# Window attention with a mixture of experts: heads transposed ahead of rows, the first slot's rows split at once, expert weights loaded from step 5

## The chip, the cores and the metric

The kernel runs on one core of a Trainium2 chip. The metric is device time in microseconds. Time before: 641.11 us, the median of three runs (640.95 to 641.42).

## The reference

Attention with a causal window of 64 positions feeds a mixture of eight experts, of which each token uses one.

```python
B, H, S, D = (8, 8, 576, 64)
scores = np.matmul(q, k.transpose(0, 1, 3, 2)) / np.sqrt(D)
scores = np.where((rel >= 0) & (rel < 64), scores, -1e9)     # rel = i - j
attn = softmax(scores)
x = np.matmul(attn, v).transpose(0, 2, 1, 3).reshape(4608, 512)
logits = x @ w_gate + modality_bias[modality_id]             # 8 experts
e_idx, gate_w = argmax(logits), max(softmax(logits))
for e in range(8):
    mask = e_idx == e
    out[mask] = gate_w[mask, None] * (np.maximum(x[mask] @ w1[e], 0) @ w2[e])
```

w1 is 512 x 1024 and w2 is 1024 x 512 for each expert, all in float32.

## The kernel before

The 4608 positions are 72 blocks of 64. A step s (0 to 35, and four more that drain) does one pair of blocks for all eight heads; two pairs make a group G, whose q and k are transposed together. The work of a pair is spread over four steps. In step s TensorE (PE) does, in this order: the values of pair s-2 (`values`, L633), the logits of pair s-3 (`logits`, L658), the scores of pair s (`scores`, L581), two transpositions of the probabilities of pair s-1 (`probs_t`), the transposition of the attention rows of pair s-2 (`x_t`, from `xa` to `xaT`), and two transpositions of heads for the next group (`heads_t`: K in even steps, Q in odd ones). All transpositions carry the line of a helper, L439. In odd steps from 5 on the routing's matrix products follow (`route2`).

VectorE (DVE) does the copy of the upper half of v (L511), the sums' reciprocal, `xa` (L641), the bias of the logits (`lg`, L663), eight masked minima (L595), the copies of the heads out of PSUM (L546), the small routing operations, which a queue hands out a few at a time (`tick`), and `split_lo` (L116). ScalarE (ACT) does the copies of the transposed probabilities (`pT`, L616), eight exponentials (L607) in three portions of two, three and three, the copy `xaT` (L650) behind the first portion, the copy of the heads K1, and `split_hi` (L111). GpSimd scatters the finished rows to DRAM by expert. SP issues nearly all loads.

From step FIRST = 12 on, the experts run between the attention's parts. Work of one expert on up to 256 rows is a slot; `slot_pieces` is a generator that yields after each piece of a slot, and `gap(it, True)` in a step takes one piece. The first two pieces of a slot transpose its rows, which come from DRAM (`x_part`, L254); then come products in float32 taken apart into a high and a low part (`first`, L279; `second`, L301). What a piece leaves to be done on ScalarE and VectorE stands in a list, `later`, and runs where `run_later()` is called: for `x_part` the split into `xh` (L192) and `xl` (L193), for `first` the split into `hh` and `hl`.

The weights of the two experts that are used first come in 32 pieces of 256 KB. Which experts these are is worked out on VectorE (`choose`, L783) and read into registers of SP (`load_weights`, L799). Each call of `weights(s)` does at most three things: the low part of the piece whose high part the call before made, the high part of the older of two loaded pieces, and the load of the next, so that two are always on their way:

```python
if halves:
    split_lo(*halves.pop(0))
if len(raws) == 2 or raws and not pieces:
    split_hi(*raws[0])
```

PSUM has banks `tp` (two), `sp0`, `sp1`, `av`, `em`, `y0` and `y1`. `turn_bank(s)` hands out the transpositions' banks: before step 12 in turn `tp`, `tp`, `em`, `y0`, `y1`, then the two `tp` alone. In step 0 a second pair of transpositions is needed for group 0 (`first_pair(1, ...)`), whose copies the scores of step 1 wait for. The k and q of groups 1 to 7 wait in a stretch of SBUF that later holds weights, and so are named `Whi` in rows.

The order is written by hand in the loop over steps: each engine works through what the loop gives it, in that order.

Of the kernel before, what the change touches and what calls it, by code (L numbers as in the profile page):

```python
# [8 lines left out]
F32 = mybir.dt.float32  # L9
# [10 lines left out]
P = 128  # L20
# [6 lines left out]
def tile_window_attn_moe(  # L27
# [12 lines left out]
    nc = tc.nc  # L40
# [8 lines left out]
    NPR = NBLK // 2  # L49
# [14 lines left out]
    FIRST = 12  # L64
# [56 lines left out]
    queue = []  # L121
# [4 lines left out]
    def tick(n=1, table=False):  # L126
        for _ in range(n):
            if routing and not table:
                routing.pop(0)()
            elif queue:  # L130
                queue.pop(0)()
                issued[0] += 1
# [94 lines left out]
    def run_later():  # L227
        while later:
            later.pop(0)()

    def fetch():
        if fetched:
            return fetched.pop(0)
        row, late, buf, whichever, need = todo.pop(0)
        assert late is not None or not pads
        assert late is None or late in scattered
        tick(need - issued[0], table=True)
        nb = 1 if whichever == NANY else 2
        return dict(xt=load_slot(row, late, nb), buf=buf, any=whichever, nb=nb)
# [191 lines left out]
    def gap(it, wait=False):  # L431

        if next(it, "end") != "end" and not wait:
            run_later()
            tick()
# [10 lines left out]
    ps_m = actx.enter_context(tc.tile_pool(name="ps_m", bufs=1, space=PSUM))  # L446
# [36 lines left out]
    def turn_bank(s):  # L483

        i = n_tp[0]
        n_tp[0] += 1
        if s < FIRST and i % 5 > 1:
            return ps_m.tile([P, 512], F32, name=("em", "y0", "y1")[i % 5 - 2])
        return ps_t.tile([P, 512], F32, name="tp")
# [45 lines left out]
    def heads_t(G, nm, i, tp):  # L535


        src = qk[G, nm].rearrange("p t (h a) d -> p t h (a d)", a=2)
        for h in range(2):
            for t in range(2):  # L540
                n = 2 * h + t
                turn(tp[:, n * P:(n + 1) * P], src[:, t, 2 * i + h])

    def heads_out(tp, G, nm, i, copy):
        dst = by_group(qT if nm == "q" else kT)[:, G % 2, 2 * i:2 * i + 2]
        copy(out=dst.rearrange("p h j (i t) -> p h t (j i)", t=2),  # L546
             in_=tp.rearrange("p (h t i) -> p h t i", h=2, t=2))
# [54 lines left out]
    def exps(p, us):  # L602
        ss, mn, sm = st[p, "s"]
        for u in us:
            a, hp = divmod(u, HP)
            h = 2 * hp + a
            nc.scalar.activation(  # L607
                out=ss[a][:, hp, :], in_=ss[a][:, hp, :], func=AF.Exp,
                bias=mn[:, h:h + 1], scale=-1.0, accum_out=sm[:, h:h + 1])
# [35 lines left out]
    def x_t(p, xp):  # L645
        xa = st[p, "xa"]
        for c in range(NC1):
            turn(xp[:, c * P:(c + 1) * P], xa[:, c * P:(c + 1) * P])
        xaT = st[p, "xT"] = work.tile([P, DM], F32, name="xaT")
        nc.scalar.copy(out=xaT, in_=xp)  # L650

    def logits(p, lt):
        G, j = divmod(p, GB)
        xaT = st.pop((p, "xT"))
        for c in range(NC1):
            for i in range(2):
                cols = slice(c * P + i * W64, c * P + (i + 1) * W64)
                nc.tensor.matmul(  # L658
                    out=lt[i * W64:(i + 1) * W64, 0:E], lhsT=xaT[:, cols], rhs=wg[:, c, :],
                    start=(c == 0), stop=(c == NC1 - 1))  # L660
        if j == 0:
            st[G, "lg"] = small.tile(sh3, F32, name="lg")
        nc.vector.tensor_tensor(  # L663
            out=st[G, "lg"][:, j, :], in0=lt[:, 0:E], in1=bias_sel[:, p, :], op=ALU.add)
# [118 lines left out]
    def choose():  # L783

        lead = []
        for m in range(2):
            c = brow[0:1, m, :]
            u, _, mx = first_max(tab, f"selb{m}", c)
            rest = stt(tab, f"rest{m}", u, -1.0e6, c, ALU.mult, ALU.add)
            less = reduce(tab, f"less{m}", rest, ALU.max)  # L790
            lead.append(tt(tab, f"lead{m}", mx, less, ALU.subtract))
            if m:
                cnt0 = ts(tab, f"cnt0_{m}", u, lead[m], ALU.mult)
                cnt0 = stt(tab, "cnt0", last_u, lead[0], cnt0, ALU.mult, ALU.add)
            last_u = u
        pick("X", 0, cnt0)
        pick("Y", 1, stt(tab, "cnt1", sel2[:, 0, :], -1.0e6, cnt0, ALU.mult, ALU.add))

        def load_weights():  # L799
            for x in range(2):  # L800
                evs.append(nc.values_load(ix2[0:1, x:x + 1], engines=[ET.SP], min_val=0, max_val=E - 1))
            pieces.extend((x, c) for x in range(2) for c in PIECE_ORDER)
        queue.append(load_weights)


    at = {}
# [52 lines left out]
    for h in range(2):  # L859
        rows = slice(h * W64, (h + 1) * W64)  # L860
# [99 lines left out]
    def weights(s):  # L960
# [5 lines that stand above are left out]
            halves.append(raws.pop(0))  # L966
        while pieces and len(raws) < 2:
            x, c = pieces.pop(0)
            raw = epool.tile([P, WCH], F32, name="y", bufs=4)
            raws.append((load_piece(raw, evs[x], c), x, c))  # L970

    for s in range(NPR + 4):
        j = s % GB
        for f, args in at.pop(s, ()):
            f(*args)
        n_tick = 6 if s < FIRST else 5
        n_gap = 0 if s < FIRST else 4
        G = s // GB + 1
        heads = PARTS[j] if G < NG else ()
        R = (s - 5) // GB if s >= 5 and j == 1 else -1  # L980
        if 1 <= s < FIRST:
            swap_upper(s - 1)

        if 2 <= s < NPR + 2:
            values(s - 2)
            values_out(s - 2)
        if 3 <= s < NPR + 3:
            logits(s - 3, turn_bank(s))
            if (s - 3) % GB == GB - 1:
                route1((s - 3) // GB)  # L990
        if s < NPR:
            scores(s)
            if s == 0:
                keep_warm(WARM[1])
            minima(s)
        if 1 <= s <= NPR:
            if s >= FIRST:
                swap_upper(s - 1)
            swap_v(s - 1)
            for a in range(2):  # L1000
                probs_t(s - 1, a, turn_bank(s))
            sums(s - 1)
        if s < NPR:
            exps(s, (0, 1))
        if n_gap > 0:
            gap(it, True)
        if 2 <= s < NPR + 2:
            x_t(s - 2, turn_bank(s))
        run_later()
        tick(2)  # L1010
        if s == FIRST - 1:
            fetched.append(fetch())
        if s < NPR:
            exps(s, (2, 3, 4))
        if s == 0:
            first_pair(1, (both[:1], both[1:]))
        if n_gap > 0:
            if s < FIRST + 4 or s % 2:
                weights(s)
            gap(it, True)  # L1020
        if heads:
            tp = turn_bank(s)
            heads_t(G, *heads[0], tp)
            heads_out(tp, G, *heads[0], nc.vector.tensor_copy)
        run_later()
        tick(n_tick)
        cnt = None
        if R >= 0:
            tp = turn_bank(s)
            rk = route2(R, tp)  # L1030
            if R == NG - 1 or any(R == T for T, _ in EARLY):
                cnt = counts_out(tab if R == NG - 1 else pl, counts(R, tp))
            route3(R, rk)
        if s < NPR:
            exps(s, (5, 6, 7))
        if n_gap > 2:
            if FIRST < s < FIRST + 3:
                weights(s)
            gap(it, True)
        if heads:  # L1040
            tp = turn_bank(s)
            heads_t(G, *heads[1], tp)
            heads_out(tp, G, *heads[1], nc.scalar.copy if heads[1] == K1 else nc.vector.tensor_copy)
        run_later()
        tick(n_tick)
        if s >= 3:
            weights(s)
        if n_gap > 3:
            gap(it, True)
        run_later()  # L1050
        if s == 0:
            choose()
        if s == 1:
            select_bias()
        if s == 4:
            nc.sync.dma_start(out=xs_blk[DUMMY:DUMMY + 2].rearrange("b p c -> p b c"), in_=padrow)
        for T, xs_ in EARLY:
            if T == R:
                plan(T, xs_, cnt)
# [120 lines left out]
    while next(it, "end") != "end":  # L1180
# [6 lines left out]
        for n in range(RAWS):  # L1187
            if n < len(swaps) and n == len(ahead) and swaps[n][0] <= t + RAWS:
                _, buf, x, c = swaps[n]
# [18 lines left out]
    with tc.If(trip > 0):  # L1208
        NS = N // P + E
        with ExitStack() as gctx:  # L1210
# [38 lines left out]
            with tc.For_i(0, trip, 1) as it:  # L1249
# [22 lines left out]
                for n in range(F // 512):  # L1272
                    tp = gps.tile([P, 512], F32, name="gxp")
# [53 lines left out]
```

## Time and profile before

| | |
|---|---|
| median of the runs | 641.11 us |
| the profiled execution | 641.34 us, its span 639.6 us |
| busy, share of the span | PE 616.7 us (96%), DVE 367.5 (57%), ACT 299.9 (47%), POOL 136.0 (21%) |
| granted clock of TensorE | 0.998 of full speed |
| DMA | 88.07 MB, mean 138 GB/s |
| scores begin | step 1: 14.48 us, step 12: 77.97, step 13: 90.62 |

The share of busy time is an average over two stages: the attention without slots, steps 0 to 11, and everything behind it. Rows of a timeline give an instruction's start, its duration, engine, line, operation and operands, and in brackets the time its engine had been idle and what ended that.

### The profile page before, as it was taken

How to read it: one execution, taken by the hardware profiler on the slowest of the kernel's cores; microseconds unless marked ns; L12 is line 12 of the kernel's file. 1: busy time of each engine (PE TensorE's matmuls, PEld its weight loads, DVE VectorE, ACT ScalarE, POOL GpSimd, SP SyncE). 2: the span in 40 equal slices, each digit the busy share in tenths (PEclk: the TensorE clock that was granted, in tenths of full speed). 3: DMA queues.
4: the chain of work that ended last, by engine and by line, in shares of the span. 5: the costliest groups of instructions: out<-in, count | busy, mean ns of one | idle time of the engine just before them, and what ended most of it. 6: DMA issues, size and time to landing. Idle time of an engine off the chain costs nothing.

```text
span 639.6 us, 17262 instructions
## 1 busy us (share of the span) xinstructions
PE 616.7 (96%) x6508; PEld 552.8 (86%) x6509; DVE 367.5 (57%) x1495; ACT 299.9 (47%) x933; POOL 136.0 (21%) x314
## 2 busy tenths in 40 slices
PE   6799889999999999999999999999999999999996
PEld 4687778989898899989888899998999889989885
DVE  2999968767677766666654364213224624667611
ACT  4799867665657555646462111111112513554411
POOL 5333232132212320321222121011001001101102
PEclk9999999999999999999999999999999999999999
DMA  9999975866677754563312026312232723678301
GB/s 162 207 233 231 187 196 132 198 171 159 149 171 176 156 134 85 133 149 85 101 50 101 34 100 244 113 41 67 61 136 78 241 79 111 204 245 242 104 1 36
DMA packets 138885, 88.07 MB, mean 138 GB/s; under 512 B 116746, under 2 KB 116784, under 8 KB 138672
## 3 DMA queue, kind: packets, MB, share of 16 engines
q1 hardware_dynamic: 130112, 67.44, 43.6%
q0 software_dynamic: 5856, 18.92, 8.0%
q10 hardware_dynamic: 2832, 0.59, 0.7%
q8 instruction: 52, 0.85, 0.6%
q14 instruction: 33, 0.27, 0.2%
HBM read 67.49 MB, written 23.91 MB: 143 GB/s over the span
## 4 chain that ended last, share of the span: by engine, by line
PE 50%; DVE 0%; ACT 0%; issue 0%; POOL 0%; POOLq 0%; ACTq 0%
PE y L301 23%; PE em L279 13%; PE sp L279 10%; PE tp L439 1%; PE y L352 1%; PE av L633 1%; PE em L254 1%; PE tp L254 1%; PE sp L327 0%; PE em L327 0%; PE tp L658 0%; PE sp L581 0%; DVE xa L641 0%; ACT ss L607 0%; POOL out_dram L365 0%
## 5 line engine op out<-in xcount | busy, mean ns | idle before, releaser
L301 PE MATMUL y<-Whi,hh 128*128 128x512 f32 x288 | 118.7, 412 | 0.0
L607 ACT ACTIVATE ss<-ss,mn 128x128 f32<-128x128 f32 x288 | 112.9, 400 | 4.5 <-DVE mn L595 4.5
L301 PE MATMUL y<-Wlo,hh 128*128 128x512 f32 x288 | 112.9, 392 | 0.0
L301 PE MATMUL y<-Whi,hl 128*128 128x512 f32 x288 | 112.8, 392 | 0.0
L279 PE MATMUL em<-xh,Whi 128*128 128x256 f32 x400 | 102.8, 291 | 1.2 <-ACT xh L192 0.7
L279 PE MATMUL em<-xh,Wlo 128*128 128x256 f32 x400 | 98.0, 279 | 0.0
L288 DVE SCALAR_TENSOR_TENSOR hl<-em,hh 128x512 fp32r<-128x512 f32 x50 | 34.5, 690 | 91.4 <-ACT hh L287 89.7
L312 POOL DMA_INDIRECT out_dram<-y,id x36 | 37.3, 1037 | 222.1 <-DVE y L309 143.6
L279 PEld LDWEIGHTS em<-xh,Whi 128*128 128x128 f32 x400 | 75.4, 188 | 2.6 <-ACT xh L192 0.9
L279 PEld LDWEIGHTS em<-xh,Wlo 128*128 128x128 f32 x400 | 75.3, 188 | 0.9
L287 ACT ACTIVATE hh<-em 128x512 fp32r<-128x512 f32 x50 | 29.6, 593 | 93.1 <-PE em L279 89.1
L595 DVE CUSTOM_DVE_ANT_0 ss<-sp,masks 128x128 f32<-128x128 f32 x288 | 63.5, 286 | 12.5 <-PE sp L581 12.5
L616 ACT COPY pT<-tp 128x512 f32<-128x512 f32 x57 | 31.7, 591 | 75.7 <-PE tp L439 75.6
L301 PEld LDWEIGHTS y<-Whi,hl 128*128 128x128 f32 x288 | 54.1, 188 | 12.3
L279 PE MATMUL em<-xl,Whi 128*128 128x256 f32 x400 | 63.0, 279 | 0.0
L301 PEld LDWEIGHTS y<-Whi,hh 128*128 128x128 f32 x288 | 54.1, 188 | 7.5
L301 PEld LDWEIGHTS y<-Wlo,hh 128*128 128x128 f32 x288 | 54.3, 188 | 7.1
L607 ACT ACTIVATION_READ_ACCUMULATOR ss<-ss,mn 128x1 f32 x288 | 56.8, 197 | 0.0
L734 POOL DMA_INDIRECT xs_scratch<-xa,idx x36 | 36.6, 1016 | 84.6 <-DVE lm L677 27.2
L279 PEld LDWEIGHTS em<-xl,Whi 128*128 128x128 f32 x400 | 53.8, 188 | 0.0
L288 DVE SCALAR_TENSOR_TENSOR hl<-sp,hh 128x512 fp32r<-128x512 f32 x22 | 15.2, 692 | 61.1 <-ACT hh L287 61.1
L287 ACT ACTIVATE hh<-sp 128x512 fp32r<-128x512 f32 x22 | 13.2, 598 | 76.6 <-PE sp L279 76.6
(247 smaller groups left out, 1263.6 us busy)
## 6 DMA issues: line engine op xcount, KB each, us to landing
xt<-xs_scratch SPq DMA_DIRECT2D x18, 514.0 KB, 3.9
vo<-in_v_dram SPq DMA_DIRECT2D x32, 256.0 KB, 5.1
y<-in_moe_w_dram SPq DMA_DIRECT2D x32, 256.0 KB, 3.9
vo<-in_moe_w_dram SPq DMA_DIRECT2D x24, 256.0 KB, 3.7
ss<-in_moe_w_dram SPq DMA_DIRECT2D x24, 256.0 KB, 3.9
xs_scratch<-xs_scratch SPq DMA_DIRECT2D x8, 514.0 KB, 5.9
pT<-in_moe_w_dram SPq DMA_DIRECT2D x16, 256.0 KB, 4.2
qk<-in_k_dram SPq DMA_DIRECT2D x14, 256.0 KB, 5.0
```

What stands on the lines that cost most here:

```text
L254: nc.tensor.transpose(out=tp[:, n * P:(n + 1) * P].bitcast(F32R), in_=xt[:, t, c * P:(c + 1) * P].bitcast(F32R), identity=ident_r)
L279: nc.tensor.matmul(out=hb[:, i * TP:(i + 1) * TP], lhsT=w[buf][:, c0:c0 + P], rhs=x[:, c * TP:(c + 1) * TP], start=(n == 0), stop=(n == le ...
L287: nc.scalar.activation(out=hh, in_=hb, func=AF.Relu),
L288: nc.vector.scalar_tensor_tensor(out=hl, in0=hb, scalar=0.0, in1=hh.bitcast(F32), op0=ALU.max, op1=ALU.subtract)))
L301: nc.tensor.matmul(out=sl["y", t], lhsT=h[:, i * TP + t * P:i * TP + (t + 1) * P], rhs=w[buf][:, c0:c0 + DM], start=(k == 0 and n == 0), s ...
L312: ins = nc.gpsimd.indirect_dma_start(out=out, out_offset=bass.IndirectOffsetOnAxis(ap=sl["id"][:, t:t + 1], axis=0), in_=y, in_offset=None ...
L352: nc.tensor.matmul(out=yp[:, cols], lhsT=sl["h", n][lo][:, c * P:(c + 1) * P], rhs=w[buf][:, c0 + cols.start:c0 + cols.stop], start=(m == ...
L439: nc.tensor.transpose(out=out_, in_=in_, identity=ident[p0:p0 + n, p0:p0 + n])
L595: nc.vector.tensor_tensor_reduce(out=ss[a][:, hp, :], in0=sp[a][:, hp * P:(hp + 1) * P], in1=mask, scale=-1.0 / 8.0, scalar=3.0e38, op0=AL ...
L607: nc.scalar.activation(out=ss[a][:, hp, :], in_=ss[a][:, hp, :], func=AF.Exp, bias=mn[:, h:h + 1], scale=-1.0, accum_out=sm[:, h:h + 1])
L616: nc.scalar.copy(out=pT, in_=pp)
L734: ins = nc.gpsimd.indirect_dma_start(out=xs, out_offset=bass.IndirectOffsetOnAxis(ap=idx[:, j:j + 1], axis=0), in_=xg[j], in_offset=None)
```

## The change

In steps 0 to 11 both transpositions of heads come ahead of the transposition of rows, right behind the transpositions of the probabilities, and `x_t` follows behind them, in the program after the second portion of exponentials; the copies out of PSUM stay where they were. In step 12 `run_later()` is called straight behind each of the slot's first two pieces, so that `xh` and `xl` are made ahead of the `xaT` copy and of the weights' splits, and the logits use the bank `y0`. The weights' registers are read at the end of step 5 and not from VectorE's queue; the calls of `weights` begin in step 5 instead of step 3, and there are three of them in each of the steps 12 to 15, where step 12 and step 15 had two.

```diff
-            logits(s - 3, turn_bank(s))
+            logits(s - 3, turn_bank(s) if s != FIRST else ps_m.tile([P, 512], F32, name="y0"))
...
             gap(it, True)
-        if 2 <= s < NPR + 2:
+        if s == FIRST:
+            run_later()
+        rows = 2 <= s < NPR + 2
+        if rows and s >= FIRST:
             x_t(s - 2, turn_bank(s))
...
+        early_heads = heads if s < FIRST else ()
+        tps = [turn_bank(s) for _ in early_heads]
+        for h, tp in zip(early_heads, tps):
+            heads_t(G, *h, tp)
         if s < NPR:
             exps(s, (2, 3, 4))
+        if rows and s < FIRST:
+            x_t(s - 2, turn_bank(s))
         if s == 0:
             first_pair(1, (both[:1], both[1:]))
         if n_gap > 0:
-            if s < FIRST + 4 or s % 2:
+            if FIRST < s < FIRST + 4 or s % 2:
                 weights(s)
             gap(it, True)
+        if s == FIRST:
+            run_later()
+            weights(s)
...
-            if FIRST < s < FIRST + 3:
+            if FIRST <= s < FIRST + 4:
                 weights(s)
...
-        if s >= 3:
+        if s == 5:
+            load_weights()
+        if s >= 5:
             weights(s)
```

On TensorE in step 0, between the products that keep it warm and the scores of step 1, the pair of group 0 is `qk` and the K heads of group 1 are `Whi_64`:

```order
-L439 MATMUL em<-ident_r,qk 128x64 x4
-L439 MATMUL y_300<-ident_r,qk 128x64 x4
-L439 MATMUL em<-ident_r,qk 128x64 x4
-L439 MATMUL y_300<-ident_r,qk 128x64 x4
-L439 MATMUL y_319<-ident_r,Whi_64 128x128 x4
-L439 MATMUL tp<-ident_r,Whi_64 128x128 x4
+L439 MATMUL em<-ident_r,Whi_64 128x128 x4
+L439 MATMUL y_297<-ident_r,Whi_64 128x128 x4
+L439 MATMUL y_309<-ident_r,qk 128x64 x4
+L439 MATMUL tp<-ident_r,qk 128x64 x4
+L439 MATMUL y_309<-ident_r,qk 128x64 x4
+L439 MATMUL tp<-ident_r,qk 128x64 x4
```

The heads of group 1 have moved ahead of the pair that step 1's scores use.

On ScalarE in step 12, from the probabilities' copies to the first product's `hh`, before:

```order
L616 COPY pT<-tp 128x512 x2
L607 ACTIVATE ss,sm<-ss,mn 128x128 x2
L650 COPY xaT<-tp 128x512
L192 CAST xh<-em 128x512
L607 ACTIVATE ss,sm<-ss,mn 128x128 x3
L111 CAST Whi_65<-y 128x512
L192 CAST xh<-tp 128x512
L681 ACTIVATE ex<-lg 128x16
L607 ACTIVATE ss,sm<-ss,mn 128x128 x3
L546 COPY kT<-tp 128x2x2x128
L111 CAST Whi_65<-y 128x512
L287 ACTIVATE hh<-em 128x512
```

and with the change:

```order
L616 COPY pT<-tp 128x512 x2
L607 ACTIVATE ss,sm<-ss,mn 128x128 x2
L192 CAST xh<-em 128x512
L650 COPY xaT<-tp 128x512
L607 ACTIVATE ss,sm<-ss,mn 128x128 x3
L192 CAST xh<-tp 128x512
L111 CAST Whi_65<-y 128x512
L681 ACTIVATE ex<-lg 128x16
L607 ACTIVATE ss,sm<-ss,mn 128x128 x3
L111 CAST Whi_65<-y 128x512
L546 COPY kT<-tp 128x2x2x128
L111 CAST Whi_65<-y 128x512
```

Each `xh` has moved one place up, the first ahead of `xaT`, the second ahead of a weight's cast, and a third cast stands in the step.

On VectorE in step 12, behind the minima, before:

```order
L193 TENSOR_TENSOR xl<-em,xh 128x512
L677 TENSOR_REDUCE lm<-lg 128x2
L678 TENSOR_TENSOR lg<-lg,lm 128x16
L116 TENSOR_TENSOR Wlo_66<-y,Whi_65 128x512
L546 COPY kT<-tp 128x2x2x128
L193 TENSOR_TENSOR xl<-tp,xh 128x512
```

and with the change:

```order
L193 TENSOR_TENSOR xl<-em,xh 128x512
L677 TENSOR_REDUCE lm<-lg 128x2
L678 TENSOR_TENSOR lg<-lg,lm 128x16
L193 TENSOR_TENSOR xl<-tp,xh 128x512
L116 TENSOR_TENSOR Wlo_66<-y,Whi_65 128x512
L546 COPY kT<-tp 128x2x2x128
```

The second `xl` has moved ahead of the weight's low part and of the heads' copy.

## Rows read from the trace of the kernel before

**Rows 1.** Busy time by stretch: us, PE, PEld, DVE, ACT, POOL, clock, DMA share, GB/s.

```profile
15.63:77.97 62.34, 54.47 (x1063) 48.31 (x1063) 58.60 (x330) 56.41 (x221) 20.69 (x41) 1.00 1.01 220
77.97:90.62 12.65, 9.54 (x137) 8.15 (x133) 9.36 (x42) 9.59 (x33) 5.20 (x10) 1.00 0.79 214
...
90.62:101.28 10.66, 10.66 (x145) 9.61 (x141) 7.94 (x36) 6.79 (x23) 0.88 (x3) 1.00 0.41 96
```

**Rows 2.** Waits of VectorE, 15.6 to 79 us: line, releaser, us in total, times, longest.

```profile
DVE ss L595 <- PE sp L581: 0.8, 1, 0.8
DVE xa L641 <- PE em L439: 0.5, 1, 0.5
DVE xa L641 <- PE tp L439: 0.3, 1, 0.3
```

**Rows 3.** Waits of ScalarE, 15.6 to 79 us, the longest.

```profile
ACT ss L607 <- DVE mn L595: 2.3, 4, 1.0
```

**Rows 4.** Waits of TensorE, 15.6 to 79 us, for xa.

```profile
PE y L439 <- DVE xa L641: 2.4, 3, 1.2
...
PE tp L439 <- DVE xa L641: 1.8, 2, 1.3
```

**Rows 5.** Timeline of TensorE in step 12 (start us, us, what, [idle before <-releaser]).

```profile
80.68 0.63 PE L439 MATMUL tp<-ident_r,ss 128*128 128x128 f32 x4 [1.00 <-DVE lg L663]
81.75 0.54 PE L254 MATMUL em<-ident_r,xt 128*128 128x128 f32 x4 [0.44 <-DMA xt<-xs_scratch]
...
83.48 0.66 PE L439 MATMUL tp<-ident_r,Whi 128*128 128x128 f32 x4 [0.43 <-ACT xaT L650]
84.69 0.39 PE L279 MATMUL em<-xh,Whi 128*128 128x256 f32 x1 [0.56 <-DVE xl L193]
...
86.11 0.38 PE L279 MATMUL em<-xh,Whi 128*128 128x256 f32 x1 [0.68 <-ACT xh L192]
...
87.18 0.60 PE L439 MATMUL tp<-ident_r,Whi 128*128 128x128 f32 x4
```

**Rows 6.** Timeline of step 0 and step 1's scores, TensorE and ScalarE.

```profile
12.06 0.69 PE L439 MATMUL em<-ident_r,qk 64*128 64x64 f32 x4
...
13.46 0.66 PE L439 MATMUL y<-ident_r,Whi 128*128 128x128 f32 x4
...
14.48 1.10 PE L581 MATMUL sp<-kT,qT 64*64 64x128 f32 x32
...
13.56 0.64 ACT L562 COPY qT<-y 128x512 f32<-128x512 f32 x1 [0.42 <-PE y L439]
```

**Rows 7.** Timeline of SP's queue, 5.5 to 6 us: issue of K's second half.

```profile
5.51 1.21 SPq L532 DMA_DIRECT2D Whi<-in_k_dram  x1
```

**Rows 8.** DMA issues of 5.5 to 6.6 us: count, KB each, us to landing.

```profile
Whi<-in_k_dram SPq DMA_DIRECT2D x1, 256.0 KB, 7.1
```

**Rows 9.** Lines L116 and L111 up to step 11 (duration ns min/median/max).

```profile
L116 DVE TENSOR_TENSOR Wlo<-y,Whi x7: 673/683/686, 42.4 to 78.9; 128x512 fp32r<-128x512 f32 x7
...
L111 ACT CAST Whi<-y x8: 609/641/663, 39.4 to 78.8; 128x512 fp32r<-128x512 f32 x8
```

**Rows 10.** Timeline of VectorE in step 12.

```profile
83.94 0.69 DVE L193 TENSOR_TENSOR xl<-em,xh 128x512 fp32r<-128x512 f32 x1 [1.26 <-ACT xh L192]
...
86.09 0.69 DVE L193 TENSOR_TENSOR xl<-tp,xh 128x512 fp32r<-128x512 f32 x1
...
89.85 0.69 DVE L288 SCALAR_TENSOR_TENSOR hl<-em,hh 128x512 fp32r<-128x512 f32 x1 [1.77 <-ACT hh L287]
```

**Rows 11.** Timeline of ScalarE in step 12.

```profile
82.84 0.59 ACT L650 COPY xaT<-tp 128x512 f32<-128x512 f32 x1
83.32 0.59 ACT L192 CAST xh<-em 128x512 fp32r<-128x512 f32 x1
...
84.58 0.39 ACT L607 ACTIVATE ss<-ss,mn 128x128 f32<-128x128 f32 x1
...
85.47 0.58 ACT L192 CAST xh<-tp 128x512 fp32r<-128x512 f32 x1
```

More of the change, by code (lines that the diff above doesn't have):

```diff
@@ L802, in load_weights @@
             pieces.extend((x, c) for x in range(2) for c in PIECE_ORDER)
-        queue.append(load_weights)
+        return load_weights
     at = {}
@@ L1017, in tile_window_attn_moe @@
         if n_gap > 0:
-            if s < FIRST + 4 or s % 2:
+            if FIRST < s < FIRST + 4 or s % 2:
                 weights(s)
             gap(it, True)
+        if s == FIRST:
+            run_later()
+            weights(s)
         if heads:
-            tp = turn_bank(s)
-            heads_t(G, *heads[0], tp)
-            heads_out(tp, G, *heads[0], nc.vector.tensor_copy)
+            if not early_heads:
+                tps = [turn_bank(s)]
+                heads_t(G, *heads[0], tps[0])
+            heads_out(tps[0], G, *heads[0], nc.vector.tensor_copy)
         run_later()
@@ L1040, in tile_window_attn_moe @@
         if heads:
-            tp = turn_bank(s)
-            heads_t(G, *heads[1], tp)
-            heads_out(tp, G, *heads[1], nc.scalar.copy if heads[1] == K1 else nc.vector.tensor_copy)
+            if not early_heads:
+                tps = [None, turn_bank(s)]
+                heads_t(G, *heads[1], tps[1])
+            heads_out(tps[1], G, *heads[1], nc.scalar.copy if heads[1] == K1 else nc.vector.tensor_copy)
         run_later()
         tick(n_tick)
-        if s >= 3:
+        if s == 5:
+            load_weights()
+        if s >= 5:
             weights(s)
@@ L1051, in tile_window_attn_moe @@
         if s == 0:
-            choose()
+            load_weights = choose()
         if s == 1:
```

## The prediction

> **What bounds the kernel now.** I read the busy time by stretch first. From step 1's minima (15.63 us) to the scores of step 12 (77.97) VectorE is busy 58.60 of 62.34 us, ScalarE 56.41 and TensorE 54.47; from step 13 on TensorE fills its stretch [rows 1]. So time can be gained before about 90 us only; what is gained there reaches the end one for one.
>
> Who sets the pace of the attention steps? The waits of each engine tell. VectorE waits three times in that stretch, 1.6 us in all, 0.8 of it at its very start, for step 1's scores [rows 2]. The rest of its idle time is the small steps between dependent operations. ScalarE waits for VectorE's minima for 2.3 us [rows 3], and TensorE waits for `xa` from VectorE in two groups of 2.4 and 1.8 us [rows 4]. So steps 1 to 11 are VectorE's queue, run end to end. What takes nothing out of that queue, or only puts TensorE's work in another order, gains nothing there; what delays its start at 15.63 is lost in full.
>
> Step 12 is different. There TensorE stops five times, 3.1 us together: 1.00 for the logits' addition, 0.44 for the slot's rows from DRAM, 0.43 for the `xaT` copy, 0.56 for `xl` and 0.68 for `xh` [rows 5]. VectorE and ScalarE have idle time in that step (9.36 and 9.59 busy of 12.65) [rows 1].
>
> **Part 1: heads ahead of rows, steps 0 to 11.** In steps 2 to 11 TensorE's waits for `xa`, 4.2 us [rows 4], are no longer in front of the heads. I count this as nothing, since VectorE waits for no heads in that stretch [rows 2]. Its own cost: the `xaT` copy stands behind three more exponentials, but the logits that need it are a step away.
>
> Step 0 pays. Before, the second pair's transposes begin at 12.06, the K heads of group 1 follow at 13.46, and scores start at 14.48 [rows 6]. Now the K heads come first, and the second half of their data is issued at 5.51 [rows 7] and lands 7.1 us later, at 12.6 [rows 8]. The heads' first transpose runs at 12.06, the second waits until about 12.6, and the seven that are left take 7/8 of the 1.02 us from 13.46 to 14.48, or 0.9 [rows 6]. The pair then begins at about 13.5. It needs 1.40 (12.06 to 13.46), ScalarE's copy of its `qT` starts 0.10 after that and takes 0.64 [rows 6]. So the scores of step 1 start at about 15.64 where they started at 14.48: 1.16 later, and with them VectorE's queue. It has one gap of 0.5 soon after, at `xa` of step 2, put down to TensorE [rows 2], which may swallow up to that much. Bounds 0.6 and 1.2; no row decides between them, so I take the middle, **+0.9 us**.
>
> **Part 2: weights from step 5.** Each call loads a piece, casts the high part of the one before and subtracts for the low part of the one before that. Starting two steps later takes two subtractions of 683 ns on VectorE and two casts of 641 ns on ScalarE out of steps 4 to 6 [rows 9]. VectorE loses 2 x 0.683 = **-1.37 us** from a queue without gaps; ScalarE's 1.28 keep it from taking the lead. SP's two register loads move from step 2 to step 5; behind them in SP's queue stand the first weight pieces and step 6's loads, and no engine waits for a landing in that stretch [rows 2 to 4], so I count nothing. The two pieces of work come back as third calls in steps 12 and 15. VectorE waits 1.26 and 1.77 us in step 12 [rows 10], which covers 0.68; at step 15 TensorE is the bound. If that cover were gone, step 12 would be up to 0.68 + 0.64 longer.
>
> **Part 3: step 12.** The logits get a bank of their own, so the second transposition of probabilities need not wait 1.00 for their addition [rows 5]. It ends at about 80.2 instead of 81.3, but behind it stands the slot's first transposition, whose rows land just before 81.75 [rows 5]; the 1.00 becomes a longer wait for the rows. What it frees is ScalarE: its `pT` copy and the two exponentials behind it come 1.0 sooner, and it is free at about 81.75 instead of just before 82.84 [rows 11]. I walk on from there with durations of [rows 5, 10, 11].
> - Slot's first transposes 81.75 to 82.29; `xh` at once, 82.33 to 82.92 (before from 83.32); `xaT` 82.85 to 83.42, as before; so the heads start at 83.48, as before.
> - `xl` 82.97 to 83.66 (before 83.94 to 84.63). The first product shares its bank with those rows and need not wait 0.56: it starts at 84.06 instead of 84.69.
> - Three exponentials of 0.4 (83.4 to 84.55), then the second `xh` to 85.1, where before a weight cast stood ahead of it and it ran from 85.47. TensorE's third chunk goes at about 85.16, not 86.11.
> - Second `xl` 85.14 to 85.83, not from 86.09. The next heads start at about 86.24 instead of 87.18.
>
> That is **-0.95 us**, and nothing else is waited for until the scores of step 13. Bounds: nothing, if the rows land later or a weight cast waits for its piece, and -3.1, if all five waits went.
>
> **Sum.** +0.9 - 1.37 - 0.95 = -1.4 us. The profiled execution took 641.34 us (span 639.6 and 1.7 around it), which gives 639.9; the median of the runs, 641.11, is 0.2 below it, so I forecast **639.7 us**. About 0.2% (1.3 us) is what a measurement of this kernel can tell from no change.
>
> **Rivals.**
> *ScalarE takes the pace.* Its queue is as long as VectorE's within 2.2 us [rows 1]. It would carry the stall in full (+1.16), gain 1.28 by the casts, and in step 12 some 0.4 of the 0.95. Sum -0.5: 640.6 us. For it: both are near full. Against: it waits 2.3 us for minima, and VectorE never for it [rows 2, 3].
>
> *Transfers set the pace.* The DMA engines' share in the stretch is 1.01 at 220 GB/s [rows 1]. Two pieces of 256 KB fewer before step 12 are then worth 0.52 MB / 220 GB/s = 2.4 us instead of 1.37; with +0.9 and -0.95 that is -2.45: 638.7 us. Against: no engine of the chain waits for a landing [rows 2 to 4]. The Trainium skill, "DMA: Bandwidth & Descriptors", Specifications, says that transfers in runs under 512 B miss line rate; by that rule the queues of this stretch, which carry q, k and v in runs of 64 floats, stay full, and it speaks for this rival. The trace agrees that the queues are full (1.01), not that anyone waits for them.
>
> *ScalarE stands at `xaT`.* The row transposes are now TensorE's last work of a step (but for the routing's counts), and the last three exponentials stand behind their copy. If TensorE reached them later than ScalarE had done its fifth exponential, the 4.2 us of waits for `xa` [rows 4] would pass to ScalarE, and from it to the next step's `pT`: +4.2 + 0.9 - 1.37 - 0.95 = +2.8, 643.9 us. It decides where two heads (1.02 us [rows 6]) and the wait for `xa` take TensorE beyond two `pT` copies and five exponentials (about 3 us at 0.6 and 0.4 each). Against: that leaves some 2 us of room, the longest single wait for `xa` was 1.3 [rows 4], and `xa` stands ahead of the minima on VectorE.
>
> **How the numbers follow.** Forecast 0.52, ScalarE's pace 0.22, transfers 0.18, `xaT` 0.08. The forecast's own bounds are 0.6 to 1.2 for the stall and about 0.5 either way for step 12: 638.9 to 640.5. The range reaches below to the transfers' case with a spread of 0.9, and above short of the last rival: 637.8 to 641.8. Faster by over 0.2% means below 639.8: just over half of the forecast's own chance, nearly all of the transfers' case, a fifth of ScalarE's, some 0.51. Slower (over 642.4) is the last rival and a little: 0.09. The rest, 0.40, is within 0.2%.
>
> **What would show it.** Right: the scores of step 1 starting near 15.6; VectorE still without gaps until step 12, and step 12 begun 0.2 to 0.8 us earlier; in step 12 TensorE's waits for the logits' addition and for `xl` gone, one longer wait for the rows, and scores of step 13 near 89.2 instead of 90.6. From there on the stretches of before. Wrong: ScalarE waiting at `xaT` for TensorE; waits for landings after step 0; a TensorE wait for a weight part in steps 13 to 16; or a step 0 without the wait for the second half of K.

## The result and the profile after

The changed kernel took 643.75 us (median of 11 runs) where the kernel before took 642.64 in the same comparison: ratio 1.0027, interval 1.0014 to 1.0039. **It is slower**, and outside the range of 637.8 to 641.8. A second comparison, with nothing edited (below), gave 648.26 against 643.02: 1.0085, 1.0058 to 1.0112. Executions of one kernel differ here by 3 us and more, for reasons that the last section takes up, so I compare stretches of the profiled executions and not totals alone.

The profiled execution of the changed kernel took 644.91 us (span 643.2, so 3.6 longer than before's). When the scores of a step begin, in us:

| step | 1 | 2 | 3 | 4 | 11 | 12 | 13 |
|---|---|---|---|---|---|---|---|
| before | 14.48 | 19.97 | 26.77 | 32.51 | 71.43 | 77.97 | 90.62 |
| after | 15.62 | 19.81 | 28.28 | 35.81 | 76.88 | 83.26 | 94.19 |
| after, second profile | 15.81 | 20.00 | 27.91 | 34.10 | 79.09 | 84.96 | 97.59 |
| rows first, bank `y1` (experiment 11) | 14.21 | 19.77 | 26.57 | 32.27 | 70.17 | 76.71 | 88.25 |

From step 13 on before and after are alike (237.0 us from there to the scores of step 35 in both). The loss is made by step 4 (+3.3 us) and between steps 4 and 11 (41.07 us, not 38.92: +2.15); steps 11 and 12 give 1.87 back (17.32, not 19.19). That sums to the 3.6. The second profile has no spell at half clock ahead of step 4 and begins that step at 34.10, so some 1.7 of the 3.3 belong to the spell of the first, at 27.0 to 33.8 us.

Busy time by stretch, after, columns as in [rows 1]: the spell at half clock in steps 2 and 3, steps 4 to 10, step 11, step 12, step 13:

```profile
27.00:33.80 6.80, 6.80 (x79) 6.45 (x75) 5.78 (x35) 3.89 (x16) 1.02 (x3) 0.50 0.67 141
35.81:76.88 41.07, 35.95 (x714) 32.72 (x711) 34.99 (x204) 36.27 (x145) 13.57 (x26) 1.00 0.93 218
76.88:83.26 6.38, 5.22 (x107) 4.79 (x104) 6.06 (x36) 6.01 (x24) 0.97 (x2) 1.00 0.30 77
83.26:94.19 10.93, 9.05 (x135) 8.14 (x132) 9.41 (x41) 9.30 (x31) 4.48 (x9) 1.00 0.59 194
94.19:104.85 10.66, 10.66 (x144) 9.61 (x141) 8.05 (x36) 6.79 (x23) 1.11 (x3) 1.00 0.71 179
```

In the second row no engine is full any more: of 41.07 us VectorE works 34.99, ScalarE 36.27, TensorE 35.95, at full clock. Before, VectorE had 3.7 us of idle time in 62 [rows 1]; now it has 6.1 in 41. So nobody's queue sets the pace; a chain across engines does. The waits of TensorE in steps 1 to 11 (those of [rows 4]):

```profile
PE tp L658 <- ACT xaT L650: 2.2, 3, 0.8
...
PE y L658 <- ACT xaT L650: 1.8, 3, 0.8
PE y L658 <- DVE tgt L715: 1.2, 1, 1.2
...
PE em L658 <- ACT xaT L650: 0.5, 1, 0.5
```

The waits for `xa` that part 1 was to take out of the way are nearly gone, and seven waits of the logits for the `xaT` copy have come, 4.5 us; the kernel before had none. VectorE (first row; before [rows 2]) and ScalarE (before [rows 3]) now wait for TensorE in turn:

```profile
DVE ss L595 <- PE sp L581: 2.6, 3, 1.0
```

```profile
ACT pT L616 <- PE em L439: 3.4, 2, 2.7
ACT pT L616 <- PE y L439: 2.8, 4, 1.2
ACT pT L616 <- PE tp L439: 2.2, 2, 1.2
ACT ss L607 <- DVE mn L595: 1.3, 2, 1.0
```

Each waits for another: a ring. One turn of it, from the timeline of after, TensorE and ScalarE, step 8:

```profile
58.71 0.64 PE L658 MATMUL y<-wg,xaT 128*64 128x8 f32 x16 [0.73 <-ACT xaT L650]
...
59.27 1.10 PE L581 MATMUL sp<-kT,qT 64*64 64x128 f32 x32
...
60.31 0.66 PE L439 MATMUL y<-ident_r,ss 128*128 128x128 f32 x4
...
61.06 0.58 ACT L616 COPY pT<-y 128x512 f32<-128x512 f32 x1 [0.73 <-PE y L439]
...
61.54 0.59 ACT L616 COPY pT<-tp 128x512 f32<-128x512 f32 x1
...
62.02 0.42 ACT L607 ACTIVATE ss<-ss,mn 128x128 f32<-128x128 f32 x1
...
63.95 0.57 ACT L650 COPY xaT<-y 128x512 f32<-128x512 f32 x1
```

The logits stand on TensorE ahead of the scores, the scores ahead of the probabilities' transposition; its copy stands on ScalarE ahead of the second one, that ahead of five exponentials, these ahead of `xaT`, and the next logits, at 64.57, wait for `xaT`. The turn is 0.56 + 1.04 + 0.75 + 0.48 + 0.48 + 1.93 + 0.62 = 5.86 us. Steps 4 to 10 take 5.86 or 5.87 us each, every one; before they took 4.87 to 6.18, on average 5.56 (38.92 / 7).

In steps 0 and 12 the change does about what it was to do. Step 0, after (before [rows 6]):

```profile
12.02 1.20 PE L439 MATMUL em<-ident_r,Whi 128*128 128x128 f32 x4
13.01 0.77 PE L439 MATMUL y<-ident_r,Whi 128*128 128x128 f32 x4
13.71 0.46 PE L439 MATMUL y<-ident_r,qk 64*128 64x64 f32 x4
...
15.62 0.65 PE L581 MATMUL sp<-kT,qT 64*64 64x128 f32 x13 [0.71 <-ACT qT L562]
```

Step 12, all waits of TensorE (before [rows 5], five of them, 3.1 us):

```profile
86.33 0.54 PE L254 MATMUL em<-ident_r,xt 128*128 128x128 f32 x4 [0.95 <-DMA xt<-xs_scratch]
88.06 0.66 PE L439 MATMUL tp<-ident_r,Whi 128*128 128x128 f32 x4 [0.44 <-ACT xaT L650]
89.69 0.39 PE L279 MATMUL em<-xh,Whi 128*128 128x256 f32 x1 [0.49 <-ACT xh L192]
```

### The profile page after: what moved, and what is told of

It reads as the page before. It is cut to its first block, busy times and chain, and to the rows that moved or that the text cites. A ratio compares the mean times of both kernels' runs of the same rounds, so it can differ in the third digit from the quotient of the medians.

```text
span 643.2 us, 17278 instructions
## 1 busy us (share of the span) xinstructions
PE 619.9 (96%) x6508; PEld 557.2 (87%) x6509; DVE 366.9 (57%) x1495; ACT 299.6 (47%) x933; POOL 136.8 (21%) x314
## 4 chain that ended last, share of the span: by engine, by line
PE 50%; DVE 0%; ACT 0%; issue 0%; POOL 0%; POOLq 0%; ACTq 0%
PE y L301 22%; PE em L279 12%; PE sp L279 10%; PE tp L439 1%; PE y L352 1%; PE av L633 1%; PE em L254 1%; PE tp L254 1%; PE sp L327 0%; PE em L327 0%; PE tp L658 0%; PE sp L581 0%; DVE xa L641 0%; ACT ss L607 0%; POOL out_dram L365 0%
## 5 line engine op out<-in xcount | busy, mean ns | idle before, releaser
L595 DVE CUSTOM_DVE_ANT_0 ss<-sp,masks 128x128 f32<-128x128 f32 x288 | 63.5, 286 | 14.9 <-PE sp L581 13.9
L607 ACT ACTIVATION_READ_ACCUMULATOR ss<-ss,mn 128x1 f32 x288 | 55.3, 192 | 0.0
L734 POOL DMA_INDIRECT xs_scratch<-xa,idx x36 | 36.5, 1013 | 84.2 <-DVE lm L677 27.2
```

Source lines behind the costliest of these rows:

```text
L595: nc.vector.tensor_tensor_reduce(out=ss[a][:, hp, :], in0=sp[a][:, hp * P:(hp + 1) * P], in1=mask, scale=-1.0 / 8.0, scalar=3.0e38, op0=AL ...
L607: nc.scalar.activation(out=ss[a][:, hp, :], in_=ss[a][:, hp, :], func=AF.Exp, bias=mn[:, h:h + 1], scale=-1.0, accum_out=sm[:, h:h + 1])
L734: ins = nc.gpsimd.indirect_dma_start(out=xs, out_offset=bass.IndirectOffsetOnAxis(ap=idx[:, j:j + 1], axis=0), in_=xg[j], in_offset=None)
```

## The experiments

Theory: the ring. Rivals: the step 0 stall, the spell at half clock, the bank of step 12. "S4 to S11" is the time from the scores of step 4 to those of step 11. The diffs are against the changed kernel unless they say otherwise.

**1. The copy early.** TensorE's order of heads and rows stays as changed, but `xaT` stands behind two exponentials instead of five.

```diff
+        if rows and s < FIRST:
+            x_t(s - 2, turn_bank(s))
         if s < NPR:
             exps(s, (2, 3, 4))
-        if rows and s < FIRST:
-            x_t(s - 2, turn_bank(s))
```

> The changed kernel with one thing put back: in steps 2 to 11 the xaT copy stands ahead of the third exponential again (TensorE's order, heads ahead of rows, stays). Theory 1 (a ring: logits wait for xaT, scores stand behind the logits, the probabilities behind the scores, then two copies, five exponentials and xaT): the ring loses three exponentials, 1.17 us of 5.87, so the even step of 5.87 us is gone, steps 4 to 11 take 5.0 to 5.6 us on average, TensorE's waits of 0.7 us for xaT ahead of the logits are gone, and the time falls by 2 to 4 us against the change. Theory 2 (the fall of TensorE's clock in steps 2 and 3 is the cost): steps 4 to 11 stay as they are, time within 0.5 us of the change. Theory 3 (the wait for K's second half in step 0 is the cost): as theory 2.

Measured: 642.05 us, ratio to before 1.0008 (0.9991 to 1.0025), so the gain against the change is some 1.2 us by the ratios (1.0027), less than the 2 to 4 expected. S4 to S11 is 38.80. TensorE's waits for `xaT` in steps 1 to 11 are gone; the longest in total are now

```profile
PE av L633 <- POOL ve L505: 4.7, 4, 1.3
PE y L658 <- DVE tgt L715: 1.2, 1, 1.2
```

The ring is open with one copy moved, and the order on TensorE by itself costs nothing there.

**4. The copy last.** The opposite: `xaT` behind all eight exponentials.

```diff
-        if rows and s < FIRST:
-            x_t(s - 2, turn_bank(s))
...
             exps(s, (5, 6, 7))
+        if rows and s < FIRST:
+            x_t(s - 2, turn_bank(s))
```

> The changed kernel with the xaT copy and its transpositions behind all eight exponentials in steps 2 to 11, the doubled dose of what theory 1 blames. Theory 1: the ring gets three exponentials longer, 1.17 us, so steps 4 to 11 take 7.0 us each and the time rises by 8 to 10 us. Theories 2 and 3: no more than 1 us, since each engine does the same work.

Measured in its one profiled execution: 660.45 us, S4 to S11 52.34, the undisturbed steps 7.02 to 7.13, where 7.0 was expected; the time rose by more than the expected 8 to 10 us. With 5.87 for five exponentials and 0.39 for one (1.93 / 5), eight give 7.04 and two 4.70. At two the ring is shorter than a step; at eight it waits longest:

```profile
PE y L658 <- ACT xaT L650: 5.9, 3, 2.0
PE tp L658 <- ACT xaT L650: 5.5, 4, 1.8
PE em L658 <- ACT xaT L650: 2.8, 2, 1.9
```

The steps above 7.13 are those in which TensorE's clock was at half; the mean granted clock from 36 to 88 us was 0.90.

**2. Rows first.** Parts 2 and 3 without part 1.

```diff
-        if rows and s >= FIRST:
+        if rows:
...
-        early_heads = heads if s < FIRST else ()
+        early_heads = ()
...
-        if rows and s < FIRST:
-            x_t(s - 2, turn_bank(s))
```

> The changed kernel without its first part: rows ahead of heads in every step, as before; the late weights and step 12's order stay. Theory 1: steps 3 to 11 at 5.4 us or less, step 12 begins 0.5 to 1.5 us earlier than in the kernel before and is 1.0 to 1.7 us shorter: 638 to 639.5 us where the kernel before takes 641. Theory 2: the same if the clock stays up; if it falls here too, 2 to 3 us more. Theory 3: the same as theory 1.

Measured: 643.09 us, ratio 1.0007 (0.9990 to 1.0024). S4 to S11 38.14, the ring's 2.9 us below after, and 0.8 below before. But step 11 took 7.65, not 6.54, and step 12 had a spell at half clock, 86.1 to 89.5; the 638 to 639.5 expected was missed.

**3. Step 12 alone.** The kernel before with part 3.

```diff
-            logits(s - 3, turn_bank(s))
+            logits(s - 3, turn_bank(s) if s != FIRST else ps_m.tile([P, 512], F32, name="y0"))
...
+        if s == FIRST:
+            run_later()
...
+        if s == FIRST:
+            run_later()
+            weights(s)
```

> The kernel before with the step-12 part alone (the logits in y0, both splits at once; two weight calls in the step as before). The prediction's walk gave 0.95 us for it; the changed kernel's step 12 is 10.94 us against 12.65. If all of that is this part's: step 12 at 10.9 to 11.0 and 1.5 to 1.7 us less than before. If some of it is the wait for the slot's rows, which shrinks when step 11 runs late: step 12 at 11.7 and 0.9 us less.

Measured: 642.70 us, ratio 1.0008 (0.9994 to 1.0022). Step 11 again 7.65, step 12 11.94 with a spell at half clock, 84.2 to 87.6, so longer than either expectation. What is gained in step 12 is lost at the end of step 11: the logits in `y0` wait for a product of the routing there, until VectorE's `tgt` has read it. It is the same new wait as in after (1.2 us, above), here 0.9.

**5 and 6. Heads alone, weights alone.** The kernel before with part 1 alone, and with part 2 alone (`load_weights` at the end of step 5, `weights` from step 5, three calls to step 15).

> The kernel before with the first part alone (heads ahead of rows and the xaT copy behind five exponentials, in steps 0 to 11). Theory 1 (the ring through xaT): steps 4 to 10 at 5.87 us each, with TensorE waiting 0.3 to 0.8 us for xaT ahead of the logits of most steps; from the scores of step 4 to those of step 11 41 us, where the kernel before takes 38.9 and the one without this part 38.1. The time 2 to 4 us above before. Rival (the loss is TensorE's lower clock in steps 2 and 3, or step 0): 38 to 39.5 us from step 4 to step 11, and any loss lies ahead of step 4.

> The kernel before with the weights' part alone (registers and calls from step 5, three calls in each of steps 12 to 15). The prediction had 1.37 us for two subtractions fewer on VectorE. In the kernel without the first part the stretch from the scores of step 4 to those of step 11 took 38.12 us against 38.92: expected here 38.1 again, so 0.8 us and not 1.37, step 11 as before at 6.5, step 12 at 12.6 plus up to 0.7 for the third call; time 0.3 to 0.8 us below before.

Measured: heads alone 651.88 us, ratio 1.0126 (1.0088 to 1.0164); weights alone 642.88, ratio 0.9990 (0.9976 to 1.0005). Part 1 alone carries the loss, and more than in after and than the 2 to 4 us expected: S4 to S11 is 44.55, its steps 5.87 or 5.88 in turn with 6.81 to 7.15. The wait that I had expected in step 0, for the second half of K, is seen here by itself:

```profile
12.58 0.90 PE L439 MATMUL em<-ident_r,Whi 128*128 128x128 f32 x3 [0.30 <-DMA Whi<-in_k_dram]
```

Weights alone leave S4 to S11 at 38.95, where 38.1 was expected. Part 3 changes nothing ahead of step 12, so experiments 2, 11 and 12 have the same instructions in this stretch, and took 38.14, 37.90 and 37.86. What differs is one wait of VectorE, for `xa` in step 7, here and in experiment 2:

```profile
52.07 0.69 DVE L641 TENSOR_TENSOR xa<-av,rs 128x512 f32<-128x512 f32 x1 [1.77 <-PE em L439]
```

```profile
51.63 0.69 DVE L641 TENSOR_TENSOR xa<-av,rs 128x512 f32<-128x512 f32 x1 [0.97 <-DMA xs_scratch<-xa,idx]
```

`xa` takes a buffer again from which GpSimd scatters rows in step 6. The first line names TensorE, but `xa` reads nothing of that transposition, and the trace has the scatter's landing at 51.95. In experiments 11 and 12 the wait is 0.67 and 0.45. In the kernel before the landing, at 49.11, came ahead of `xa`, at 49.79. Less the wait the four stretches are 37.2 to 37.4 us (an estimate, since it takes the wait as uncovered).

**7 and 8. Bank `y1`.** Experiment 8 is the changed kernel with step 12's logits in `y1`; experiment 7 adds the early copy and the old order in step 0.

```diff
-ps_m.tile([P, 512], F32, name="y0")
+ps_m.tile([P, 512], F32, name="y1")
```

> The changed kernel with three things altered: the xaT copy ahead of the third exponential (as in the first run), step 0's heads behind its second pair as before, and the logits of step 12 in y1 and not in y0, whose last reader is VectorE's tgt of step 11. Theory 1: no 5.87 us steps, 38.0 to 38.8 us from step 4 to step 11; step 11 loses the 1.2 us wait for tgt ahead of the logits, so 5.9 us, but step 12 keeps its gate, the slot's rows, and takes 11.5 to 12; the scores of step 13 come 1.5 to 2.5 us earlier than in the kernel before if TensorE's clock rises at the same time in the first steps. Time 1 to 2 us below before.

> The changed kernel with the logits of step 12 in y1 instead of y0. The wait of 1.2 us for tgt ahead of the logits goes. If it was uncovered, the scores of step 13 follow those of step 11 by 16.1 us instead of 17.3. If the slot's rows from DRAM are the gate, TensorE waits 2 us for them instead of 0.9, and the distance stays at 17.0 to 17.3.

Measured: experiment 7 642.52 us, ratio 1.0003 (0.9980 to 1.0026), with runs from 639.69 to 646.81; in its profile S4 to S11 is 37.96, step 11 6.31, and the scores of step 13 begin at 88.89, 1.7 ahead of before. The wait for `tgt` is gone; the 1 to 2 us expected below before do not show in the median. Experiment 8, one profiled execution, is a miss: 652.00 us, S4 to S11 46.21, S11 to S13 20.16. Its instructions up to step 11 are those of after, and yet its steps take 5.88 to 7.39: spells at half clock (two of them in steps 11 and 12, so the distance expected there is not tested), and late starts of ScalarE's copies, of which the next experiment shows one.

**9. After, once more.**

> The changed kernel itself once more, with nothing edited: a second profile of the same instructions. Theory (ring through `xaT`): steps 4 to 10 again take 5.87 us each or longer, never less, so the scores of step 11 stand at least 41.0 us behind those of step 4, whatever TensorE's clock does before. Rival (the two spells of half clock at 27.0 to 33.8 us made the loss): without such spells the stretch is 38 to 39.5 us, as before.

Measured: 648.26 us (ratio above). No spell of half clock at 27 to 34, and still S4 to S11 is 44.99: its seven steps take 5.87, 5.87, 5.95, 5.87, 7.30, 7.39 and 6.75, none less than a turn of the ring. So the spells in steps 2 and 3 made after's loss no more than partly; the ring is there in every profile with the copy behind five exponentials. Step 8 is the one of 7.30. From its timeline:

```profile
58.69 0.66 PE L439 MATMUL y<-ident_r,ss 128*128 128x128 f32 x4
...
60.06 0.60 PE L439 MATMUL em<-ident_r,Whi 128*128 128x128 f32 x4
...
60.87 0.59 ACT L616 COPY pT<-y 128x512 f32<-128x512 f32 x1 [2.16 <-PE em L439]
60.93 0.29 DVE L595 CUSTOM_DVE_ANT_0 ss<-sp,masks 128x128 f32<-128x128 f32 x1 [0.69 <-PE em L439]
```

The transposition that both wait for ends at 59.35 by the profile, yet both start 1.5 us later. The ring has no slack, so the step is 1.43 longer (7.30 - 5.87). After it TensorE's clock fell, from 65.1 to 68.5, and step 9 became 7.39. Steps 8 and 9:

```profile
57.66:64.96 7.30, 5.16 (x105) 4.62 (x101) 5.94 (x31) 5.14 (x22) 3.84 (x6) 1.00 1.02 237
64.96:72.34 7.38, 6.78 (x108) 6.26 (x104) 5.39 (x31) 5.85 (x23) 0.42 (x2) 0.77 0.63 146
```

**10. Old order in step 0.**

```diff
-        early_heads = heads if s < FIRST else ()
+        early_heads = heads if 0 < s < FIRST else ()
```

> The changed kernel, but step 0 keeps the old order (pair ahead of heads). Theory: scores of step 1 at 14.3 to 14.6 us where the full clock begins before 13 us, up to 16 where it begins late; from step 4 to step 11 the ring's 41.0 us or more, so the time is that of the changed kernel less at most 1.2 us: 642 to 644. Rival (the order of step 0 made the loss): S4 to S11 as before, 38 to 39.5, and 639 to 641.

Measured: 648.73 us, ratio 1.0092 (1.0059 to 1.0126). Scores of step 1 at 14.15, of step 3 at 26.69, 1.7 and 1.2 earlier than in experiment 9. Not all of that is step 0's order, since the full clock began at 12.0 us here and at 13.9 there. And S4 to S11 is 43.05 and the time no better than after's; my 642 to 644 was too low, since I had counted the ring at its shortest. The rival, that step 0 made the loss, falls.

**11 and 12. Rows first, bank `y1`.** Experiment 2 with `y1`, run twice.

> The changed kernel with rows ahead of heads as before, and the logits of step 12 in bank 1 in place of bank 0. Theory: no ring, S4 to S11 38.0 to 38.4; without the wait for the routing's `tgt` step 11 takes 6.2 to 6.7 (7.65 with bank 0), step 12 10.9 to 12.1; scores of step 13 at 88.6 to 90 where the clock begins as early as before, 1 to 2 us ahead of before: 639 to 640.5, and up to 2.5 us more where it begins late. Rival (step 12's gain is given back at step 11 in any bank): step 11 above 7, step 13 at 90.6 and 641.

> The version with rows first and the logits of step 12 in bank 1, once more, with nothing edited. If its gain is its own, its runs stand about 1 us below those of before again (ratio 0.997 to 0.9995), S4 to S11 at 37.9 to 38.2 and S11 to S13 at 18.1 where the clock does not fall. If the first comparison was luck of the runs, the ratio is 1.000 or above.

Measured: 641.49 us, ratio to before 0.9981 (0.9963 to 0.9998), and 641.69, 0.9989 (0.9972 to 1.0005). This is the fastest version, some 0.15% below before; one of the two intervals ends just below 1, the other takes 1 in, so the gain is not clear of noise. The median of experiment 11 lies above the expected 639 to 640.5, within the 2.5 us allowed for a clock that begins late. In the profiles (639.65 and 639.29 us) S4 to S11 is 37.90 and 37.86, S11 to S13 18.08 and 18.10. The stretches of the first, steps 4 to 10, 11 and 12:

```profile
32.27:70.17 37.90, 35.34 (x714) 31.92 (x710) 35.57 (x202) 36.38 (x147) 13.63 (x26) 1.00 0.97 235
70.17:76.71 6.54, 5.20 (x107) 4.59 (x103) 6.11 (x37) 5.52 (x21) 0.42 (x2) 1.00 0.75 161
76.71:88.25 11.54, 9.05 (x136) 8.14 (x133) 9.93 (x43) 9.93 (x34) 4.52 (x9) 1.00 0.60 185
```

From step 13 to step 35 both take 0.6 to 0.8 us longer than before's 237.0. The second profile shows where, in steps 16 and 17:

```profile
PE tp L439 <- DVE lg L663: 0.7, 2, 0.5
```

It is not the bank's doing: experiment 6, which keeps the banks of before, has the same row. No run tells what in the weights' part brings it.

## Why the prediction was wrong

**The step that failed** is the sentence of part 1: "the `xaT` copy stands behind three more exponentials, but the logits that need it are a step away". They are a step away in the program. On TensorE they stand ahead of that next step's scores, and these ahead of the transposition that ScalarE's next copy waits for. So the moved copy closed a ring of 5.87 us, counted as nothing, in a stretch whose steps took 5.56. Nothing kept this from being worked out before. The logits' time stands in the trace of the kernel before, in step 8:

```profile
59.23 0.59 PE L658 MATMUL y<-wg,xaT 128*64 128x8 f32 x16
```

With 1.10 for the scores [rows 6], 0.63 for a transposition [rows 5], 0.59 for each of three copies and 0.39 for each of five exponentials [rows 11] that is some 6.0 us by durations, which overlap a little, for 5.87 from start to start. I saw the reader of the moved copy and the step it stands in, and did not ask where it stands in TensorE's queue and what waits behind it there. Cost: 2.9 us between steps 4 and 11 (41.07 against 38.14 in experiment 2) at its shortest; in experiment 9, with a late start and a fall of the clock on top, 6.9.

**The rival at `xaT`** gave 643.9 us, and 643.75 was measured. That is luck. The place was right, the mechanism not: it had ScalarE waiting at `xaT` for TensorE, and ScalarE never waits there; TensorE waits for ScalarE's copy. The 4.2 us it counted have nothing to do with the 2.9. I gave it 0.08 because I tested only that direction.

**Step 0** came out at 15.62 for the scores of step 1, where 15.64 was forecast, but not by the working. In after TensorE does not wait for the second half of K, which the prediction had named as a sign of being wrong. Its heads end later than the forecast 13.5, at 13.71, because they ran slowly (1.20 us for four transposes; the full clock is on record from 13.3 us only), and the pair then took less than the 1.40 that I had read from rows that are in part slow themselves: it takes 1.14 in experiment 10, from 11.99 to 13.13. The two errors cancel. Where the wait for K showed it was 0.18 to 0.30 (experiments 1, 4, 5). Between profiles whose full clock began at about the same time the scores of step 1 are 0.9 later (15.06 in experiment 8, 14.15 in 10) and 1.2 (15.27 in 4, 14.04 in 12). What VectorE's gap swallows of it stays open: experiments 9 and 10 differ by 1.66 at step 1 and 1.22 at step 3, but their clocks began 1.9 us apart. So +0.9 is neither shown nor refuted.

**Weights**, -1.37: the mechanism was right where VectorE sets the pace, but a wait was left out. Experiments 2, 11 and 12 gained 0.8 to 1.1 between steps 4 and 11, experiment 6 nothing. Less the wait for the scatter (0.45 to 1.77) all four stand 1.5 to 1.8 below before's 38.92 (which has 0.3 of waiting for TensorE in it), so the saving is there; VectorE, now earlier, reaches `xa` of step 7 before the scatter has landed and gives part or all of it back. In the changed kernel it is worth nothing that shows, since VectorE has idle time there and steps 4 to 10 take the ring's 5.87 with the weights' part or without it (experiment 5).

**Step 12**, -0.95: mechanism and size held. Its waits for the logits' addition and for `xl` are gone, and the wait for the rows is longer, 0.95 for 0.44. Experiments 11 and 12 gain 1.1 in steps 11 and 12. What I missed is that the new bank has a reader of its own in step 11: with `y0` the wait moved from the transposition to the logits (1.2 us in after, and step 11 at 7.65 in experiments 2 and 3). I looked at who fills the bank in step 12, not at who empties it before.

**Heads ahead of rows**, counted as nothing, are worth nothing: with the copy early S4 to S11 is 38.80 and 37.96 (experiments 1 and 7), rows first 38.14 and 37.90 (2 and 11).

**Transfers and ScalarE's pace** did not come as the rivals had them: after step 0 no engine of the ring waited for a load's landing before step 12, with DMA at 0.93 of its time. But a landing after step 0, a sign of being wrong, was waited for: the scatter's, at `xa` in step 7. In after that wait is 1.5 us and costs nothing, since step 7 takes 5.87 like its neighbours; with rows first it is what takes back the weights' gain. The rule of the Trainium skill, "DMA: Bandwidth & Descriptors", Specifications, that transfers under 512 B miss line rate, agrees with full queues (share 0.93 at 218 GB/s) and decided nothing here, since no engine waited for the loads that it speaks of.

## What to carry to other kernels

When an instruction is moved back on an in-order engine, follow its reader to that reader's place in its own engine's queue, and on from there until you come back to the engine you started on; if you do, add up the loop and compare it with the step, not with busy time. A loop longer than the step sets the pace with every engine part idle, and has no slack left for any other delay. When a tile goes to another bank, look at who read that bank last. When work is taken out of a queue, look at what the queue then reaches too early: here a buffer that a scatter was still reading.

## What the runs showed that I had not expected

TensorE's speed at the start differs between executions of the same instructions. Before and experiment 6 have the same program through step 1; in before four 128x128 transposes of step 0 took 0.66 us, in experiment 6

```profile
13.64 1.11 PE L439 MATMUL y<-ident_r,Whi 128*128 128x128 f32 x4
14.55 1.06 PE L439 MATMUL tp<-ident_r,Whi 128*128 128x128 f32 x4
15.54 1.99 PE L581 MATMUL sp<-kT,qT 64*64 64x128 f32 x32
```

and the scores of step 1 came at 15.54 instead of 14.48. The records of the granted clock show the full level from 11.5 us in the earliest profile (experiments 4 and 12) and from 19.9 in the latest (experiment 5). Differences of this kind, some 2 us, are as large as all that the parts of this change gain; a single time could have shown any of them faster or slower.

Later falls to the lower level, 1.2 GHz, came in every profile with the ring (after from 27.0 to 33.8 us, experiment 9 from 65.1 to 68.5) and in experiments 2, 3 and 7, but not in before, 1, 6, 11 and 12. TensorE had idle time ahead of each that I looked at (5.16 of 7.30 us busy in step 8 of experiment 9, 8.85 of 11.38 ahead of 27.0 in after), but so it had elsewhere without a fall (8.64 of 11.52 from 14.48 on in before).

What stays open is the late start of experiment 9's copy, 1.5 us behind the modelled end of the transposition. ScalarE and VectorE start within 0.06 us of each other there, so what is late is TensorE's release and not one of its readers. Such late starts, of 0.5 to 1.5 us, came in experiments 5, 8, 9 and 10, all in even steps, where K's heads are transposed behind the probabilities, but not in the same ones each time; after's first profile had none, and smaller ones, up to 0.8, came with rows first too. No run tells what holds the release back.
